# When the weight requests of the last two batches are issued, in an attention and soft-MoE kernel

## The chip, the core and the metric

The kernel runs on one core of a Trainium2 chip. The metric is the time of one execution on the device in microseconds (us). Engines named below: PE (TensorE: matrix products and transposes), DVE (VectorE), ACT (ScalarE), POOL (GpSimd), and SP (SyncE, which here only issues DMA requests). DMA requests issued by SP go to a queue that the profile calls q1, those issued by POOL to one called q0; both queues are served by the same 16 DMA engines.

## The reference

```python
# attention: B = 8 batches, H = 8 heads, S = 576 tokens, D = 64; 16 beacon keys/values ahead of the 576
scores = scale * q @ concat([beacon_k, k]).T          # causal mask on the 576, none on the beacons
a = softmax(scores);  attn = a @ concat([beacon_v, v])
# soft MoE over all N = 4608 tokens: Dm = 512, E = 8 experts x 4 slots, F = 1024
x = attn as [N, 512]
logits = x @ phi                                       # [N, 32]
d = softmax of logits over the tokens;  slot_input = d.T @ x      # [32, 512]
slot_out[e] = relu(slot_input[e] @ w1[e]) @ w2[e]
c = softmax of logits over the slots;   out = c @ slot_out        # [N, 512]
```

No expert can start before the attention of all 4608 tokens is done, since the slot inputs are sums over all tokens. The weights `w1` and `w2` are float32 in HBM, 2 MB each per expert, 33.5 MB in all; they do not depend on the attention and can be loaded at any time ahead of it.

## The kernel before, in words

**Pairs of heads.** The attention is written out as 32 pairs of heads, `n` = 0 to 31; `b, g = divmod(n, 4)` gives the batch and the pair in it. Two pairs form a half batch `m`; its keys and queries come in as two tiles `kstag` and `qstag` (L344, `load_qk`, one DMA of 576 KB each), are transposed on PE (`trps`, L492, for the very last half batch L496) and copied by DVE to `kT` and `qT`. One iteration of the loop at L759 issues, in an order written by hand for every engine (`manual_schedule`): four `scores` blocks of pair `n` (PE L523, exponentials on ACT L528, the causal mask on POOL, L514), the transposes of the next half batch, `attend` and `normalize` of pair `n-1`, and at fixed places the transposes of `x`, the logits and the slot sums of earlier batches. In the pairs with `g` = 1, 2, 3 the values of the next batch are cast (`cast_v`, POOL), and at `g` = 3 they are brought into their order in `vh`: POOL copies the last 80 tokens from `vrem` (L398), `perm_v` runs on PE, ACT (L411) and DVE, and POOL copies the beacons from `bvst` (L414).

**Loads of the inputs.** SP issues them two batches ahead: at `g` = 0 the values and the first half batch of keys and queries, at `g` = 2 the remainder of the values (`vrem`) and the second half batch, and one batch ahead the beacon values (`bvst`). Each waits for its buffer. The last of them, for batch 7, are requested in batches 5 and 6.

**Weights.** POOL issues them, since they are cast to 16 bits on the way. The list `wchunks` (L420) cuts `w1` and `w2` into 32 pieces of 512 KB (as 16 bits): both matrices of experts 0 to 4 first (20 pieces, resident in `w1h` and `w2h`), then `w1` of experts 5 to 7 (six), then `w2` of experts 5 to 7 (six). Experts 5 to 7 go into buffers that attention no longer needs: `wv` (expert 5) takes those of the values, `wt` (experts 6 and 7) those of the keys and queries. The very last piece is requested in two halves. `load_weights(count)` (L449) issues the next `count` pieces; it stands at the end of each pair (L798) and once more behind the loop (L801), where it issues whatever is left, after a POOL memset of the tile `siz`. POOL works in order, so a request stands behind every POOL instruction of its pair: the masks, the casts, and in the pairs with `g` = 3 the two copies into `vh`.

**After the pairs.** The last pair's `attend`, the last logits, the last slot sums; then the experts: `first(eg, fh)` (L829, `hps`, needs `w1`), `turn`, `second` (L850, `so`, needs `w2`), each for experts 0 to 3 and then 4 to 7. `second` of experts 4 to 7 uses the pieces of `w2` in the order of the list, the last piece last. Then `so1` is scaled by DVE (L874) and ACT (L877), and the output is computed and stored: `fps` on PE (L925), evictions on ACT (L930) and DVE (L932), DMA on SP (L936).

Of the kernel before, what the change touches and what calls it, by code (L numbers as in the profile page):

```python
# [268 lines left out]
def kernel(  # L269
# [118 lines left out]
    def cast_v(b, c):  # L388

        if c == 0:  # L390
            st["c", b] = work.tile([P, 4, H, D], F16, name="vc", tag="vc", bufs=1)
        if c < 2:
            for hs in (slice(4 * c, 4 * c + 2), slice(4 * c + 2, 4 * c + 4)):
                (nc.vector if c == 1 and b == 0 else nc.gpsimd).tensor_copy(  # L394
                    out=st["c", b][:, :, hs, :].rearrange("p t h d -> p h t d"),
                    in_=st["v", b][:, hs, :, :])
        else:
            nc.gpsimd.tensor_copy(out=vhs[b % 2][0:80, 4, :, 0:D], in_=st["r", b][0:80, :, :])  # L398
# [28 lines left out]
    def piece(e, m, j):  # L427

        if e < NRES:
            if m == 0:  # L430
                return w1h[e][:, 2 * j:2 * j + 2, :].rearrange("p t f -> p (t f)")
            return w2h[e][:, 4 * j:4 * j + 4, :].rearrange("p c d -> p (c d)")
        if (e, m, j) not in wtail:
            if e == NRES:
                t = stv.tile([P, 2, 2048], F16, name="wv", tag="v", bufs=2)
                for i in range(2):
                    wtail[e, m, i] = t[:, i, :]
            else:
                t = stq.tile([P, 2048], F16, name="wt", tag="kq"[len(wtail) % 2])
                wtail[e, m, j] = t[:, :]  # L440
        return wtail[e, m, j]
# [7 lines left out]
    def load_weights(count):  # L449
        for _ in range(count):  # L450
            if not wchunks:
                return
            e, m, j = wchunks.pop(0)
            if m == 0:
                nc.gpsimd.dma_start(
                    out=piece(e, m, j),
                    in_=moe_w1[e, 2 * j * P:2 * (j + 1) * P, :].rearrange("(p t) f -> p (t f)", t=2))
            else:
                src = moe_w2[e].rearrange("(p c) d -> p c d", c=NFC)
                cs = 2 if (e, m, j) == WLAST else 4  # L460
                for c in range(0, 4, cs):
                    nc.gpsimd.dma_start(
                        out=piece(e, m, j)[:, c * Dm:(c + cs) * Dm],
                        in_=src[:, 4 * j + c:4 * j + c + cs, :].rearrange("p c d -> p (c d)"))
# [10 lines left out]
    def transposes(m, which):  # L475

        b, hb = divmod(m, 2)
        t = st["kq"[which], b, hb]
        if which == 1:
            qTs[m] = work.tile([P, 2, S], BF, name="qT", tag="qT")  # L480
            dst = qTs[m][:, :, :]
        else:
            if m:
                beacon_keys(m)
            dst = kTs[m % 2][:, :, Nb:Nb + S]
        for j0, j1 in ((0, 5), (5, NJ)):
            tp = ps_tr.tile([P, j1 - j0, P], BF, name="trps", tag="tr")
            for j in range(j0, j1):
                for hh in range(2):
                    lo, hi = 64 * hh, 64 * hh + 64  # L490
                    if m < 2 * B - 1:
                        nc.tensor.transpose(tp[lo:hi, j - j0, :],  # L492
                                            t[:, hh, j, :].bitcast(BF)[:, 1::2], idb[:, :])
                        continue
                    for u in range(2):
                        nc.tensor.transpose(tp[lo:hi, j - j0, 64 * u:64 * u + 64],  # L496
                                            t[lo:hi, u, j, :].bitcast(BF)[:, 1::2],
                                            idb[lo:hi, lo:hi])
            do = dst.rearrange("p u (s j) -> p u s j", j=NJ)[:, :, :, j0:j1]
            ti = tp[:, :, :].rearrange("p j (u s) -> p u s j", u=2)  # L500
            if j0 and m == 0:
                nc.scalar.activation(do, ti, AF.Copy)
            else:
                nc.vector.tensor_copy(out=do, in_=ti)  # L504
# [12 lines left out]
    def scores(n, bank, masked=True):  # L517
        base, w, mms = BANKS[bank]
        sc = ps_sc.tile([P, 2, 512], FP, name="sc", tag="sc")
        for (c, q0, qw, col) in mms:  # L520
            for hh in range(2):
                po = 64 * hh
                nc.tensor.matmul(sc[:, hh, col:col + qw],  # L523
                                 kTs[n // 2 % 2][po:po + D, n % 2, c * P:(c + 1) * P],
                                 qTs[n // 2][po:po + D, n % 2, q0:q0 + qw], start=True,
                                 stop=True)
        ex = exps[n % 2]
        nc.scalar.activation(ex[:, :, base:base + w], sc[:, :, 0:w], AF.Exp, scale=scale)  # L528
        if masked:
            select(n, bank)  # L530
# [3 lines left out]
    def attend(n, hh):  # L534
        b, g = divmod(n, NG)
        h = head(n, hh)
        if hh == 0:
            pool, tag = (ps_av, "av") if n < NPAIR - 1 else (ps_sc, "sc")
            avs[n] = pool.tile([P, 2, 512], FP, name="av", tag=tag)
        av = avs[n][:, hh, 0:NC5 * DD].rearrange("p (i d) -> p i d", d=DD)  # L540
        for i in range(NC5):
            for c in range(i + 1):
                o = BLK[c, i]
                nc.tensor.matmul(av[:, i, :], exps[n % 2][0:KW[c], hh, o:o + P],  # L544
                                 vhs[b % 2][0:KW[c], c, h, :],
                                 start=(c == 0), stop=(c == i))
# [19 lines left out]
    def x_transposes(n):  # L566
        b, t = divmod(n, NG)
        tp = ps_tr.tile([P, S], F16, name="xtps", tag="tr")
        for i in range(NC5):
            nc.tensor.transpose(tp[:, QLO[i]:QLO[i] + QW[i]],  # L570
                                xs[b][0:QW[i], i, 2 * t:2 * t + 2, :].rearrange(
                                    "p h d -> p (h d)"),
                                idh[0:QW[i], 0:QW[i]])
        if n == NPAIR - 2:
            nc.scalar.activation(xT[:, t, 0:S], tp[:, :], AF.Copy)
        else:
            nc.vector.tensor_copy(out=xT[:, t, 0:S], in_=tp[:, :])  # L577
# [67 lines left out]
    def combine_T(b):  # L645

        dT = dTs[b]
        tp = ps_tr.tile([P, S], F16, name="etps", tag="tr")
        for i in range(NC5):
            nc.tensor.transpose(tp[:, QLO[i]:QLO[i] + QW[i]],  # L650
                                dT[0:QW[i], i, :, :].rearrange("p g s -> p (g s)"),
                                idh[0:QW[i], 0:QW[i]])
        nc.vector.tensor_copy(out=eT[:, b * S:(b + 1) * S], in_=tp[:, :])
# [25 lines left out]
    with tc.manual_schedule(engines={ET.PE, ET.DVE, ET.Activation, ET.Pool, ET.SP}):  # L679
# [79 lines left out]
        for n in range(2, NPAIR):  # L759
            b, g = divmod(n, NG)  # L760
            scores(n, 0)
            scores(n, 1)
            if n == 2:
                cast_v(1, 0)
            if n // 2 + 1 < 2 * B:
                transposes(n // 2 + 1, n % 2)
            attend(n - 1, 0)
            scores(n, 2)
            if n >= 3:
                x_transposes(n - 3)  # L770
            attend(n - 1, 1)
            if n >= 7 and g == 3:
                combine_T(b - 1)
            normalize(n - 1)
            scores(n, 3)
            if n == NPAIR - 1:
                x_transposes(n - 2)
            if b and g == 2:
                logits(b - 1)
            if n >= 8 and g == 0:  # L780
                dispatch(b - 2)
            if b + 1 < B and g:
                if b or g > 1:
                    cast_v(b + 1, g - 1)
                if g == 3:
                    perm_v(b + 1)
            if b + 1 < B and g == 0:
                load_bv(b + 1)
            if b + 2 < B:
                if g == 0:  # L790
                    load_v(b + 2)
                    load_qk(b + 2, 0)
                if g == 2:
                    load_vr(b + 2)
                    load_qk(b + 2, 1)
            if n == 5:
                nc.vector.tensor_copy(out=phih[:, :, :], in_=phif)
            load_weights((0, 1, 1, 1)[g] if b < 6 else 2)  # L798
        siz = work.tile([P, NDC, E * (NSL + SPE)], F16, name="siz", tag="qT")
        nc.gpsimd.memset(siz[:, :, :], 0.0)  # L800
        load_weights(len(wchunks))  # L801
# [174 lines left out]
```

## Time and profile before

| | before |
|---|---|
| median of 3 runs | 204.98 us (204.69 to 206.35) |
| the profiled execution: its own time | 204.81 us |
| its span in the profile | 203.1 us |
| PE, DVE, ACT, POOL busy | 78%, 66%, 66%, 59% of the span |
| DMA queue q1 (inputs and output): bytes, share of 16 engines | 38.01 MB, 52.9% |
| DMA queue q0 (weights): bytes, share of 16 engines | 16.78 MB, 41.5% |
| last matmul before / first transpose after the longest idle time of PE | 132.85 us / 142.38 us |
| first expert matmul (`hps`), end of `so`, end of span | 164.65, 173.85, 203.1 us |

All places in time are microseconds from the start of the span. The profile lists, for every engine, when it was busy and what ended each idle time before an instruction; the chain of work that ended last follows the program back from its end, at each step to what released it. A DMA request has an issue (on SP or POOL) and a landing, when its last part has arrived; its bytes move on 16 engines at once. The granted clock is the share of full speed at which PE was allowed to run.

### The profile page before, as it was taken

The numbers are of one execution on the slowest core, as the hardware profiler recorded it, in microseconds if no ns is written. First come the engines' busy times: TensorE is split into PE (matmuls) and PEld (weight loads), VectorE is DVE, ScalarE is ACT, GpSimd is POOL, SyncE is SP. The second block draws the span as 40 slices with busy tenths as digits, with TensorE's granted clock in tenths as the row PEclk, the third lists the DMA queues.
The fourth block names the chain that finished last, engine by engine and source line by source line (L and its number), as shares of the span: only waits on it lengthen the run. The fifth ranks groups of instructions, "written<-read, shape, count | busy, mean of one in ns | idle before, by whom it ended". The sixth has DMA issues, their size and how long they took to land.

```text
span 203.1 us, 7482 instructions
## 1 busy us (share of the span) xinstructions
PE 158.8 (78%) x3176; PEld 108.8 (54%) x3176; DVE 133.6 (66%) x281; ACT 134.1 (66%) x173; POOL 119.0 (59%) x269
## 2 busy tenths in 40 slices
PE   6687787898898989889889898900988999993300
PEld 2434555685675865667567586500867767741100
DVE  3446768888878987888887898710573733697400
ACT  2357868888888887898888888740289322692400
POOL 7028696697597588669759778801568600592000
PEclk9999999999999999999999999975599999997855
DMA  6999999999999999999999999995299994299992
GB/s 209 295 312 385 342 388 278 293 354 254 291 393 257 279 343 303 278 305 335 263 290 371 264 278 261 231 214 118 33 214 216 212 207 70 109 425 422 418 414 94
DMA packets 30646, 55.95 MB, mean 275 GB/s; under 512 B 8240, under 2 KB 16460, under 8 KB 30604
## 3 DMA queue, kind: packets, MB, share of 16 engines
q1 hardware_dynamic: 25564, 38.01, 52.9%
q0 software_dynamic: 4752, 16.78, 41.5%
q10 hardware_dynamic: 288, 0.59, 0.9%
q8 instruction: 27, 0.44, 0.8%
q14 instruction: 15, 0.12, 0.2%
HBM read 62.71 MB, written 9.44 MB: 355 GB/s over the span
## 4 chain that ended last, share of the span: by engine, by line
PE 57%; DMA 26%; ACT 7%; DVE 1%; issue 1%; POOL 1%; ACTq 0%; DVEq 0%; POOLq 0%
DMA kstag<-in_k_dram 20%; PE av L544 13%; PE sc L523 13%; PE trps L492 7%; PE xtps L570 5%; DMA out_dram<-osb 4%; ACT expT L528 4%; ACT vh L411 3%; PE fps L925 2%; PE vps L408 2%; PE lgps L589 2%; PE hps L833 2%; DMA qstag<-in_q_dram 2%; PE sips L628 2%; PE so L850 2%; PE vpt L408 1%
## 5 line engine op out<-in xcount | busy, mean ns | idle before, releaser
L528 ACT ACTIVATE expT<-sc 128x992 f16<-128x992 f32 (+3 forms) x128 | 104.7, 867 | 28.9 <-PE sc L523 28.1
L514 POOL TENSOR_SCALAR_AFFINE_SELECT expT<-expT 128x224 f16<-128x224 f16 (+3 forms) x128 | 55.1, 443 | 24.9 <-ACT expT L528 23.8
L523 PE MATMUL sc<-qT,kT 64*128 64x80 bf16 (+4 forms) x576 | 43.9, 247 | 10.7 <-ACT expT L528 5.8
L544 PE MATMUL av<-vh,expT 128*128 128x65 f16 (+1 forms) x960 | 40.8, 195 | 0.3 <-issue 0.3
L504 DVE COPY kT<-trps 128x640 bf16<-128x640 bf16 (+1 forms) x31 | 22.7, 773 | 21.9 <-PE trps L492 11.6
L544 PEld LDWEIGHTS <-expT 128*128 128x128 f16 (+1 forms) x960 | 34.1, 99 | 3.9 <-issue 1.1
L523 PEld LDWEIGHTS <-kT 64*128 64x128 bf16 x576 | 17.2, 96 | 27.7 <-issue 21.7
L504 DVE COPY qT<-trps 128x640 bf16<-128x640 bf16 (+1 forms) x31 | 22.7, 773 | 8.0 <-PE trps L492 6.3
L558 DVE TENSOR_TENSOR x<-av,r 128x640 f16<-128x640 f32 x32 | 26.4, 825 | 1.1
L394 POOL CAST vc<-vstag 128x512 f16<-128x512 f32 x30 | 17.9, 626 | 3.1 <-PE fill L664 3.1
L577 DVE COPY xT<-xtps 128x576 f16<-128x576 f16 x31 | 14.2, 457 | 5.0 <-PE xtps L570 5.0
L930 ACT ACTIVATE osb<-fps,rc 128x512 f32<-128x512 f32 (+1 forms) x19 | 11.5, 682 | 5.3 <-PE fps L925 4.2
L570 PE MATMUL xtps<-idh,x 128*128 128x128 f16 (+2 forms) x160 | 14.0, 218 | 0.1
L932 DVE TENSOR_SCALAR osb<-fps,rc 128x512 f32<-128x512 f32 (+1 forms) x18 | 12.2, 725 | 2.0 <-PE fps L925 1.3
L416 DVE CAST vh<-vpt 128x512 f16<-128x512 f32 x16 | 10.3, 685 | 2.9 <-PE vpt L408 2.9
L570 PEld LDWEIGHTS <-x 128*128 128x128 f16 (+2 forms) x160 | 9.1, 98 | 5.2 <-issue 4.9
L492 PE MATMUL trps<-idb,kstag 128*64 128x128 bf16 x270 | 10.7, 222 | 1.4 <-DMA kstag<-in_k_dram 1.4
L471 POOL COPY kT<-bkA 64x32 bf16<-64x32 bf16 x32 | 7.4, 231 | 7.0 <-DVE bkA L731 6.0
L925 PE MATMUL fps<-so,eT 128*128 128x512 f16 (+1 forms) x37 | 10.9, 421 | 0.5 <-DVE so L874 0.4
L492 PE MATMUL trps<-idb,qstag 128*64 128x128 bf16 x270 | 10.7, 222 | 0.8 <-DVE vh L416 0.5
L411 ACT ACTIVATE vh<-vps 128x1024 f16<-128x1024 f32 x8 | 8.2, 1027 | 4.6 <-PE vpt L408 4.6
L408 PE MATMUL vps<-vc,sel 32*128 32x512 f16 x64 | 9.6, 378 | 1.5 <-issue 0.8
(101 smaller groups left out, 193.1 us busy)
## 6 DMA issues: line engine op xcount, KB each, us to landing
kstag<-in_k_dram SPq DMA_DIRECT2D x15, 576.0 KB, 16.1
qstag<-in_q_dram SPq DMA_DIRECT2D x15, 576.0 KB, 14.1
out_dram<-osb SPq DMA_DIRECT2D x11, 768.0 KB, 8.8
vstag<-in_v_dram SPq DMA_DIRECT2D x7, 1024.0 KB, 11.8
w1h<-in_moe_w_dram POOLq DMA_DIRECT2D x10, 512.0 KB, 8.6
w2h<-in_moe_w_dram POOLq DMA_DIRECT2D x10, 512.0 KB, 8.5
wt<-in_moe_w_dram POOLq DMA_DIRECT2D x7, 512.0 KB, 8.1
wv<-in_moe_w_dram POOLq DMA_DIRECT2D x4, 512.0 KB, 10.6
```

The lines of the kernel that those rows point to most:

```text
L394: (nc.vector if c == 1 and b == 0 else nc.gpsimd).tensor_copy(out=st["c", b][:, :, hs, :].rearrange("p t h d -> p h t d"), in_=st["v", b][ ...
L408: nc.tensor.matmul(outs[c], sel[32 * c:32 * c + 32, t, :], vc[32 * c:32 * c + 32, t, :, :].rearrange("p h d -> p (h d)"), start=(t == 0), ...
L411: nc.scalar.activation(vhs[b % 2][:, 0:2, :, 0:D], ps[:, :, :].rearrange("p c (h d) -> p c h d", d=D), AF.Copy)
L492: nc.tensor.transpose(tp[lo:hi, j - j0, :], t[:, hh, j, :].bitcast(BF)[:, 1::2], idb[:, :])
L504: nc.vector.tensor_copy(out=do, in_=ti)
L514: nc.gpsimd.affine_select(out=ap, in_=ap, compare_op=AL.is_ge, fill=0.0, base=cbase, pattern=pat, channel_multiplier=-1)
L523: nc.tensor.matmul(sc[:, hh, col:col + qw], kTs[n // 2 % 2][po:po + D, n % 2, c * P:(c + 1) * P], qTs[n // 2][po:po + D, n % 2, q0:q0 + qw ...
L528: nc.scalar.activation(ex[:, :, base:base + w], sc[:, :, 0:w], AF.Exp, scale=scale)
L544: nc.tensor.matmul(av[:, i, :], exps[n % 2][0:KW[c], hh, o:o + P], vhs[b % 2][0:KW[c], c, h, :], start=(c == 0), stop=(c == i))
L558: nc.vector.tensor_tensor(out=xs[b][:, :, head(n, 0):head(n, 1) + 1:head(n, 1) - head(n, 0), :].rearrange("p i h d -> p h i d"), in0=av[:, ...
L570: nc.tensor.transpose(tp[:, QLO[i]:QLO[i] + QW[i]], xs[b][0:QW[i], i, 2 * t:2 * t + 2, :].rearrange("p h d -> p (h d)"), idh[0:QW[i], 0:QW ...
L925: nc.tensor.matmul(f[:, 0:hw], row_tokens(bb, j), so1[:, hw * i:hw * i + hw], start=True, stop=True)
```

## The change

One expression at the end of the loop over pairs:

```diff
-            load_weights((0, 1, 1, 1)[g] if b < 6 else 2)
+            load_weights((0, 1, 1, 1)[g] if b < 6 else (1, 1, 1, 2)[g] if b == 6 else 2)
```

Batches 0 to 5 are as before: no request behind a batch's first pair, one behind each other, 17 by the end of batch 5 (the loop begins with the third pair of batch 0). In batch 6 (pairs 24 to 27) there were two behind each pair; now there are one, one, one and two. In batch 7 (pairs 28 to 31) there are two behind each pair, as before. Before, the list was empty after one request behind pair 31 (piece 32, in its two halves). Now 30 pieces are requested by the end of the loop, and the two that remain are issued by `load_weights(len(wchunks))` at L801, behind the memset of `siz`, which found nothing left before. The order of the pieces, their sizes, their buffers and everything else are unchanged.

## The prediction

> **What bounds the kernel now.** I read the chain that ended last in order of time, then the waits of 100 to 150 us, then the DMA queues by stretch, then POOL's timeline.
>
> ```profile
> 110.30 0.58 PE trps L492 x17
> 110.89 31.45 DMA kstag<-in_k_dram
> 142.38 1.17 PE trps L496 x36
> ```
>
> Up to 110 us the chain is PE work in regular pairs: the key transposes of pair 24 start at 115.64 us, pair 25's query transposes at 119.41, so 3.77 us a pair. Then one load takes over, the last `kstag` (second half of batch 7), which was 31.45 us on its way. PE ends its last matmul ahead of it at 132.85 and stands still until 142.38.
>
> ```profile
> PEld L496 <- DMA kstag<-in_k_dram: 9.8, 1, 9.8
> POOL vh L398 <- DMA vrem<-in_v_dram: 7.6, 1, 7.6
> POOL vh L414 <- DMA bvst<-in_beacon_v_dram: 4.4, 1, 4.4
> ```
>
> POOL stands too: its two copies into `vh` wait for `vrem` (landed 139.06) and `bvst` (landed 144.0), and behind them stand pair 27's weight requests. All three loads are SP's, queue q1, requested by 118.7 us. What they shared the engines with is in the DMA queues of 128:132 (first pair of lines), 138:140 (second), 142:144 and 148:152 (one each):
>
> ```profile
> q0 software_dynamic: 197, 0.73, 90.2%
> q1 hardware_dynamic: 154, 0.19, 16.1%
> ...
> q0 software_dynamic: 88, 0.31, 77.7%
> q1 hardware_dynamic: 6, 0.01, 1.2%
> ...
> q1 hardware_dynamic: 25, 0.04, 4.9%
> ...
> q0 software_dynamic: 233, 0.83, 104.3%
> ```
>
> q0, the weights, fills the engines, and q1 creeps. The semaphore records tell how: fifteen of `kstag`'s sixteen completion steps are in by 128.6 us, the last comes at 142.3. So one DMA engine is far behind. On it the queues take turns: in 138:140 q1 gets 6 packets in 2 us, one per 0.33 us, and a 4096-byte weight packet takes 0.31 us (0.83 MB in 4 us over 16 engines). `vrem` is 640 runs of 256 bytes, 40 an engine, and each waits for a weight packet: 40 x 0.33 = 13.2 us, which is the way from 125.9 (the load ahead of it landed) to 139.06. When the weights stop, at 141 on this engine, q1 sends 2304-byte packets every 0.09 us.
>
> **The change part by part.** I number the weight pieces in their order; 17 are requested before batch 6. A piece is 0.524 MB, and 148:152 moves 0.83 MB in 4 us, so 2.5 us a piece with nothing beside it. Of POOL's requests before:
>
> ```profile
> 124.28 0.55 POOL L462 DMA_DIRECT2D w2h<-in_moe_w_dram  x1
> 124.82 0.54 POOL L455 DMA_DIRECT2D wv<-in_moe_w_dram  x1
> ...
> 128.65 0.55 POOL L455 DMA_DIRECT2D wv<-in_moe_w_dram  x1
> 129.19 0.54 POOL L455 DMA_DIRECT2D wt<-in_moe_w_dram  x1
> ...
> 144.10 0.61 POOL L414 CAST vh<-bvst 16x512 f16<-16x512 f32 x1 [4.43 <-DMA bvst<-in_beacon_v_dram]
> 144.66 1.08 POOL L455 DMA_DIRECT2D wt<-in_moe_w_dram  x2
> ```
>
> Before, pieces 18 to 23 went out with pairs 24 to 26 (119.4 to 129.2), and 24 to 32 from 144.66 on. Now 18, 19, 20 go out with pairs 24, 25, 26, pieces 21 and 22 behind pair 27's copies, and 23 to 30 two to a pair; 31 and 32 (32 is two requests of half size) follow pair 31 and the `siz` memset, 1.08 us, which before came after them.
>
> *Requests.* 33 of 0.54 us before and after; none is removed. POOL has three fewer (1.6 us) among pairs 24 to 26, where its idle gaps are 0.2 to 0.4 us before selects that wait for ACT; PE's pace is not POOL's there, so nothing to gain or lose. No new wait is written in the code. The memset moves forward; its reader is the DVE write at 163 us: nothing.
>
> *The late loads.* Pieces 21 to 23 leave the engine ahead of q1: 24 packets of 0.31 us, 7.4 us. If the engine never runs dry of weights, `bvst` lands at 144.0 - 7.4 = 136.6 and `kstag` at 135.0. But it does run dry. Piece 18 is done there near 125.2; piece 19 is now requested at 124.28, piece 20 at 128.65, and a request moves its first bytes 1.25 us later (144.66 to 145.91). Taking turns from 125.5: piece 19's eight packets take eight of `vrem`'s along (8 x 0.33, to 128.2). Then q1 is alone to 129.9: the 30 or so packets left of `vrem` at about 0.03 (0.33 less a weight packet) are 0.9 us, and in the other 0.8 go nine of `kstag`'s 16 at 0.09. Its last seven take turns with piece 20, 7 x 0.40: `kstag` lands near 133. The 16 of `qstag` behind it are 1.4 us, so `bvst` lands at 134.5. I take 133 for `kstag`, and for `bvst` 135, a little towards the bound.
>
> *Attention.* Pair 28 starts at 133.0 instead of 142.38: 9.4 us (bounds 7.4 and 9.5; PE is free at 132.85). The next pair also took 5.92 us (142.38 to 148.30) because the granted clock was 0.50 from 134.5 to 148; at 3.77 that is 2.15 more. PE would reach the last second-layer pieces (173.16 before) at 161.6, 11.5 earlier. What is late next is the weights.
>
> *The end of the weights.* POOL's copy of `bvst` now ends near 135.6, and pieces 21, 22 go out at 135.7 (floor 133.6: ACT's L411 ends at 132.42, the copy takes 0.61; ceiling 137.4, from `bvst` at 136.6). Before, nine pieces took from the request at 144.66 to the last landing at 171.0 (second half of piece 32, requested 160.05, 10.9 us): 26.3 us. Twelve take 3 x 2.47 more, 33.7. So the last weights land at **169.4**, only 1.6 us earlier (bounds 167.3 and 171.1). POOL's later requests stay ahead: pairs 28 to 31 ask by 149, the last at 151, while pieces flow to 169. Pieces 21 to 26, needed by the first layer near 156, land by about 154. So PE now waits in L850, where before it waited for no weights.
>
> *The rest.* Behind the last landing stand 13 of the L850 matmuls. Before, 88 took 2.54 us, 0.029 each; I take half clock, 0.058, as PE will have idled: 0.75 plus 0.27 for one to finish, so PE ends L850 at 170.4 against 173.85: **-3.4 us**. Bounds: at full clock -3.8; floor and ceiling of the restart move it by -2.1 and +1.7.
>
> *Output.* From there the kernel is bound by its stores, 0.79 MB each 1.9 us (425 GB/s), 0.62 us a tile of 256 KB. Even with `fps` at 0.43 us a tile PE keeps ahead; only the first tiles come later, **+0.3** (between 0 and 0.6).
>
> On the clock, the row first: PE went idle at 132.85 and the granted clock fell at 134.5, 1.7 us later, and it was back at 148.1, 5.7 us after work resumed. The Trainium skill, "TensorE: Matmul & The Clock Gate", Part 1: The HAM clock gate, speaks of an idle window of about 3.4 us before the clock halves. By that page, waits of 2.5 us from piece to piece would leave the clock full, and the sum would be -3.8 instead of -3.1. The row decides against it: 1.7 us was enough.
>
> **Sum.** -3.4 + 0.3 = -3.1 us on the profiled execution: 204.81 (span 203.1) becomes 201.7. The median of the runs is 204.98, 0.17 above it; I forecast **201.7**.
>
> **The rivals.**
>
> *The weights' tail overtakes (slower).* Three more pieces now stand behind the `bvst` wait, 7.4 us of q0 time at the end. If `bvst` does not come early enough, PE waits longer than it gained. The two balance when the last weights land at 172.5 (1.3 us before the old end), so when pieces 21, 22 go out at 138.8, `bvst` landing at 138.2. If `bvst` moved only half as far as the 7.4 us (140.3, as it would if the lagging engine were held by something other than the weights, such as the 16 KB instruction fetch on q8), the tail lands at 174.7: 207.0; if it did not move, 210.7. For: one engine alone is late, and no view says why. Against: q1's pace of one packet per weight packet, 0.33 us, and 0.09 us as soon as the weights stop. 0.10.
>
> *The change doesn't do what it says (same).* The late engine catches up 5 us and loses them at the end, between the two cases: 203 to 206, at 204.5. For: the DMA work is only moved, and both kernels end with the same bytes. Against: before, q0 stood idle from 142 to 146 while POOL waited, and the output could not start until 174. 0.12.
>
> *PE's chain decides (much faster).* If the weights kept up, the end moves by the full 11.5 us: 193.5. It needs twelve pieces in some 26 us, 2.2 us each; no stretch of the trace passes 0.86 MB in 4 us (2.44 us a piece). 0.03.
>
> *The forecast*, 199.6 (restart at its floor) to 203.5 (at its ceiling): 0.75.
>
> **How the numbers follow.** The range takes the forecast's bounds and reaches some way into the "same" case: 199.2 to 204.3. One per cent, 2 us, is about what a measurement of this kernel can tell from no change (three runs span 204.69 to 206.35). Faster by over 1%: nearly all of the forecast, 0.73, and 0.03; within 1%: 0.02 and 0.12; slower 0.10.
>
> **What the profile after would show.** Right: the wait PEld L496 on `kstag` shrinks from 9.8 us to under 2.5; L398 waits for no `vrem`; L414's wait ends near 135; the granted clock stays at 1.0 around 135 to 148; first `hps` near 153.6 instead of 164.65; a new wait of PE L850 on a DMA of `wt`, several us, and a half clock there; the last `wt` at 168 to 170.5; the stores still 425 GB/s. Wrong if: `kstag` is still late by 5 us or more with the weights gone; the pieces flow slower than 2.5 us; POOL blocks on a request because more than five are under way (the most seen before), and its selects come late; or the output at half clock falls behind its stores.

## The result, and the profile after

The changed kernel takes 202.17 us (median of six runs, 200.62 to 203.0) against 204.62 us for the kernel before beside it (six runs, 204.19 to 206.35): a ratio of 0.9864, 95% interval 0.9817 to 0.991. The profiled execution took 200.62 us (span 198.9) where that of before took 204.81 (203.1).

On two later chips the comparison came out at 1.0193 (1.0067 to 1.0319) and 1.0202 (1.0113 to 1.0292), so 2% slower, because it counts only executions near a kernel's fastest, and the kernel before has some there at 195 to 200.5 us beside about as many at 202.6 to 207.1. By medians these two chips have 201.62 us for the changed kernel against 201.24 and 200.75 against 202.82: no gain on the one, 1% on the other. What that spread is made of is the larger part of this study.

Where the time went in the profiled execution is in the waits and the chain that ended last. First the waits of the changed kernel (engine and line, what it waited for, us in total, times, longest):

```profile
PE so L850 <- DMA wt<-in_moe_w_dram: 3.2, 3, 1.7
```

The waits for `kstag`, `vrem` and `bvst` are gone, and this one is new. POOL's timeline around pair 27 (start, duration, what, idle time ahead and what ended it):

```profile
131.50 0.61 POOL L398 CAST vh<-vrem 80x512 f16<-80x512 f32 x1
132.60 0.61 POOL L414 CAST vh<-bvst 16x512 f16<-16x512 f32 x1 [0.49 <-ACT vh L411]
133.16 1.08 POOL L455 DMA_DIRECT2D wv<-in_moe_w_dram  x2
```

The DMA queues of 128:132 (two lines) and 132:136 (one; packets, MB, share of 16 engines):

```profile
q0 software_dynamic: 173, 0.64, 87.9%
q1 hardware_dynamic: 120, 0.11, 9.4%
...
q0 software_dynamic: 112, 0.39, 60.0%
```

q1 is empty by 132, and q0 runs with gaps for a few microseconds, until the new requests move. In POOL's timeline, POOL no longer stands: its copies follow ACT, and the weight requests of pair 27 go out at 133.16 instead of 144.66. Pair 28's key transposes start at 132.97 instead of 142.38. The end of the chain (start, duration):

```profile
150.72 0.95 POOL wt L462 x2
151.68 16.68 DMA wt<-in_moe_w_dram
168.40 0.60 PE so L850 x5
169.02 0.49 DVE so L874
```

Now the last half piece of the weights, requested at 151.68 and landed at 168.4, ends the experts. By stretch (length, busy time of PE, PEld, DVE, ACT, POOL with counts; then granted clock, DMA share, GB/s):

```profile
133.00:138.00 5.00, 5.00 (x165) 4.28 (x164) 3.98 (x8) 4.02 (x6) 4.42 (x11) 1.00 0.76 137
...
163.00:168.00 5.00, 2.07 (x43) 1.22 (x32) 0.00 (x0) 0.00 (x0) 0.00 (x0) 0.86 0.57 107
168.00:173.00 5.00, 4.51 (x31) 2.38 (x30) 2.47 (x4) 2.76 (x5) 2.97 (x2) 0.50 0.16 62
```

PE works through 133 to 138, where it stood before, at full clock. From 163 it waits for weights instead, and the output starts at half clock.

### The profile page after: what moved, and what is told of

Read it like the earlier page. It is cut to its first block, busy times and chain, and to the rows that moved or that the text cites. A ratio compares the mean times of both kernels' runs of the same rounds, so it can differ in the third digit from the quotient of the medians.

```text
span 198.9 us, 7482 instructions
## 1 busy us (share of the span) xinstructions
PE 161.8 (81%) x3176; PEld 108.6 (55%) x3176; DVE 133.8 (67%) x281; ACT 134.2 (67%) x173; POOL 118.5 (60%) x269
## 4 chain that ended last, share of the span: by engine, by line
PE 63%; DMA 14%; ACT 8%; DVE 3%; issue 2%; POOL 2%; ACTq 0%; DVEq 0%
PE av L544 16%; PE sc L523 15%; PE trps L492 9%; DMA wt<-in_moe_w_dram 8%; PE xtps L570 6%; PE fps L925 5%; ACT expT L528 4%; DMA kstag<-in_k_dram 4%; ACT vh L411 4%; PE vps L408 3%; PE vpt L408 2%; PE lgps L589 2%; DMA qstag<-in_q_dram 2%; PE sips L628 2%; DVE osb L932 2%
## 5 line engine op out<-in xcount | busy, mean ns | idle before, releaser
L523 PE MATMUL sc<-qT,kT 64*128 64x80 bf16 (+4 forms) x576 | 43.1, 244 | 10.8 <-ACT expT L528 5.9
L544 PEld LDWEIGHTS <-expT 128*128 128x128 f16 (+1 forms) x960 | 33.5, 97 | 4.8 <-issue 2.0
L925 PE MATMUL fps<-so,eT 128*128 128x512 f16 (+1 forms) x37 | 12.1, 456 | 0.4 <-ACT osb L930 0.2
L894 POOL TENSOR_SCALAR lo<-so 128x512 f32<-128x512 f16 x1 | 1.5, 1508 | 16.0 <-ACT so L877 16.0
L492 PEld LDWEIGHTS <-qstag 128*64 128x64 bf16 x270 | 8.4, 110 | 4.3 <-issue 4.2
## 6 DMA issues: line engine op xcount, KB each, us to landing
vstag<-in_v_dram SPq DMA_DIRECT2D x7, 1024.0 KB, 11.9
```

The lines of the kernel that those rows point to most:

```text
L492: nc.tensor.transpose(tp[lo:hi, j - j0, :], t[:, hh, j, :].bitcast(BF)[:, 1::2], idb[:, :])
L523: nc.tensor.matmul(sc[:, hh, col:col + qw], kTs[n // 2 % 2][po:po + D, n % 2, c * P:(c + 1) * P], qTs[n // 2][po:po + D, n % 2, q0:q0 + qw ...
L925: nc.tensor.matmul(f[:, 0:hw], row_tokens(bb, j), so1[:, hw * i:hw * i + hw], start=True, stop=True)
```

## The experiments

Two quantities decide below, and this table has them for every profiled execution. "Ahead" is the number of weight pieces requested in pairs 24 to 26, or at the start of 27, so ahead of POOL's copies; "end of `so`" is the start of L874 (L876 or L877 where the edit shifts lines). A load has landed when the last of its sixteen completion steps is in.

| kernel | ahead | `kstag` landed | `bvst` landed | last `wt` landed | end of `so` | time |
|---|---|---|---|---|---|---|
| before, in the prediction | 6 | 142.3 | 144.0 | 171.0 | 173.9 | 204.81 |
| before_again | 6 | 130.6 | 140.7 | 167.5 | 171.8 | 202.74 |
| before_third | 6 | 142.0 | 143.6 | 170.2 | 174.8 | 205.69 |
| keys_first | 6 | 126.5 | 141.6 | 168.5 | 173.0 | 204.0 |
| before_early | 8 | 126.4 | 136.3 | 164.0 | 165.3 | 196.17 |
| five_ahead | 5 | 138.6 | 140.2 | 169.7 | 171.3 | 202.24 |
| four_ahead | 4 | 136.7 | 138.4 | 170.4 | 170.8 | 201.75 |
| the changed kernel | 3 | 127.8 | 131.9 | 168.4 | 169.0 | 200.62 |
| after_again | 3 | 128.8 | 134.8 | 169.4 | 170.1 | 201.82 |
| after_third | 3 | 125.0 | 130.4 | 167.6 | 168.3 | 199.92 |
| without_last_three | 3 | 131.5 | 136.9 | 163.8 | 169.3 | 200.17 |
| early_request | 5 | 129.8 | 134.0 | 168.1 | 168.6 | 200.0 |
| early_third | 5 | 128.9 | 137.5 | 169.6 | 170.1 | 201.02 |
| none_ahead | 0 | 124.7 | 126.2 | 172.9 | 173.6 | 205.26 |

More pieces ahead go with later loads: `bvst` lands at 126.2 with none ahead, at 130.4 to 136.9 with three, at 138.4 and 140.2 with four and five that are requested behind the pairs, and at 140.7 to 144.0 with six. before_early, with eight, is the exception.

### Is the late `kstag` always there? (before_again)

The kernel before, unchanged.

> The kernel before, unchanged, for a second profile. Theory (weight packets hold up q1 on the one DMA engine that is furthest behind): the last kstag again lands at 140 to 144 us, with its last completion step more than 8 us behind the other fifteen, and PE waits 8 to 11 us for it. Rival (a late engine was a chance of that one execution): the landing differs by more than 3 us, the last step is not alone, and the time is the same anyway, so that the stall of PE is not what sets it.

Measured: 202.74 and 205.41 us. In the profile `kstag` lands at 130.6 and PE does not wait for it at all. The last completion step is 4.6 us behind the fifteenth, not more than 8: that expectation missed. Yet the time is only 2 us less. The waits of that profile say why:

```profile
POOL vh L414 <- DMA bvst<-in_beacon_v_dram: 7.6, 1, 7.6
...
PE av L544 <- POOL expT L514: 4.9, 2, 4.0
```

`bvst` is late (140.7, its fifteenth step at 136.0). POOL stands at its copy, and the causal masks of pair 28, which come later in POOL's order, are not done: PE's `attend` waits for them. So the price of the late loads does not need PE to wait for a load; POOL hands it on.

### Is it vrem's small packets that hold up kstag? (keys_first)

```diff
-                    load_vr(b + 2)
-                    load_qk(b + 2, 1)
+                    load_qk(b + 2, 1)        # for the last batch only
+                    load_vr(b + 2)
```

> The kernel before, but SP requests the last key and query loads ahead of the last vrem. Nothing of the weights is changed. Theory: the 40 small packets of vrem no longer stand ahead of kstag, each of which cost one weight packet of 0.33 us, so kstag lands about 13 us earlier, near 129, and PE starts pair 28 at 133 with no wait; but vrem and bvst land as late as before (139 to 144), so POOL's copies into vh end at 144.7 as before, PE then waits for vh in pair 29 (7 us), the weights restart at 144.7 and the last lands at 171: 202 to 204 us, at most 1.3% faster than before. Rival (the load is late because its engine is slow, whatever stands ahead of it): kstag lands at 139 or later, 204.6 us.

Measured: 204.61 us (204.0 to 205.17), beside 203.4 for the kernel before (196.57 to 206.45). PE has no wait for `kstag` (126.5, ahead of the 129 expected), and `vrem` and `bvst` land at 141.5 and 141.6:

```profile
POOL vh L398 <- DMA vrem<-in_v_dram: 11.2, 1, 11.2
...
PE av L544 <- POOL expT L514: 8.8, 2, 8.0
```

Some load is late in either order. That the order decides which one is not shown: `kstag` was on time in before_again too, with the order unchanged. PE's wait of 9.5 us for keys came back as 8.8 us for masks, and nothing was won: the expected 202 to 204 was too good, because I had counted the wait for `vh` and not the masks behind it.

### How many pieces may stand ahead? (five_ahead, four_ahead, none_ahead)

```diff
-            load_weights(... (1, 1, 1, 2)[g] if b == 6 else 2)
+            load_weights(... (2, 2, 1, 2)[g] if b == 6 else 2)     # five_ahead
+            load_weights(... (2, 1, 1, 2)[g] if b == 6 else 2)     # four_ahead
+            load_weights(... (0, 0, 0, 3)[g] if b == 6 else 3)     # none_ahead
```

> Two, two, one and two requests behind the pairs of batch 6: pieces 18 to 22 ahead of pair 27's copies, so one fewer than before and two more than in the changed kernel. Theory (each piece ahead costs the late loads 2.5 us, each piece behind costs the tail 2.5 us): against the changed kernel's profile kstag lands 5 us later, near 132.8, bvst near 137, POOL restarts at 137.6, ten pieces instead of twelve remain, so the last weights land near 168 and the time is that of the changed kernel within 1 us: 201 to 202.5. Rival (the loads are late as soon as the requests leave q0 no gap, however many pieces): kstag at 138 to 141, 203.5 to 205.

Measured: 200.91 us (200.36 to 202.24), beside 203.4 for the kernel before; about the time of the theory but not its landings: `kstag` at 138.6, `bvst` at 140.2, as the rival had it. The waits:

```profile
PEld L496 <- DMA kstag<-in_k_dram: 6.1, 1, 6.1
POOL vh L398 <- DMA vrem<-in_v_dram: 5.8, 1, 5.8
...
POOL vh L414 <- DMA bvst<-in_beacon_v_dram: 2.5, 1, 2.5
```

The last three completion steps of `kstag` come together here (138.0, 138.5, 138.6): it is not always one DMA engine that lags.

> Two, one, one and two requests behind the pairs of batch 6: one piece more ahead of pair 27's copies than in the changed kernel, eleven behind them instead of twelve. Theory: bvst lands up to 2.5 us later than in the changed kernel and the tail is one piece (2.5 us) shorter behind it: the time of the changed kernel within 1 us, 200.5 to 203. Rival (more distance of the requests is what counts, each piece less ahead is a gain): slower than the changed kernel by 1 us or more.

Measured: 201.28 us (200.41 to 202.02), beside 201.62 for the changed kernel on that chip: the same within 1 us, as expected. `bvst` landed 3.6 us later than in the changed kernel's profile beside it (138.4 and 134.8), where up to 2.5 was expected, and PE waits 4.7 us for `kstag`. Here the two paths meet, the one over POOL's copy and the one over the last weights:

```profile
POOL vh L414 <- DMA bvst<-in_beacon_v_dram: 6.2, 1, 6.2
...
PE so L850 <- DMA wt<-in_moe_w_dram: 0.6, 1, 0.6
```

> No request behind the first three pairs of batch 6 and three behind each from pair 27 on: fifteen pieces stand behind POOL's copies, none ahead. Theory (the tail of the weights is the price of the change): kstag, vrem and bvst land before 131, POOL restarts at its floor near 133, PE waits for no load of attention, and the last wt lands 15 x 2.5 us and 5 us behind the restart, near 176: 207 to 210, slower than the kernel before. Rival (less weight traffic beside the late loads is good without a price): 199 to 203.

Measured: 204.78 and 205.26 us, where the changed kernel has 201.62 and the kernel before 201.24 beside it, in the median; 3.4 us above the changed kernel. The loads land early (`bvst` at 126.2, all of its sixteen steps within 3.2 us), POOL asks for weights at 131.87, and nothing of attention waits for a load. Fifteen pieces behind that take 41.1 us, to 172.9. This is the mechanism of the prediction's slower rival, shown: pieces moved behind the copies come back at the end, here at 2.0 to 2.4 us each (41.1 us for fifteen against 33.9 to 35.2 for the changed kernel's twelve). The expected 176 was too late: it stood on a restart (POOL's first weight request behind its copies) at 133 and on 43 us for the tail. POOL's requests held something new:

```profile
142.44 0.56 POOL L462 DMA_DIRECT2D wv<-in_moe_w_dram  x1
143.03 0.53 POOL L462 DMA_DIRECT2D wt<-in_moe_w_dram  x1
145.64 0.53 POOL L462 DMA_DIRECT2D wt<-in_moe_w_dram  x1 [2.08 <-DMA wv<-in_moe_w_dram]
...
155.40 0.53 POOL L462 DMA_DIRECT2D wt<-in_moe_w_dram  x1 [1.91 <-DMA wt<-in_moe_w_dram]
155.92 1.08 POOL L800 MEMSET siz<- 128x1152 f16 x1
```

The request at 145.64 goes out when the piece requested eight earlier has landed (145.4), and so do the later ones (147.97 after 147.7, 150.41 after 150.1). With eight weight requests under way POOL stands at the ninth. The trace shows why: the weight requests use eight semaphores in turn, and each request waits on the semaphore that the one eight ahead of it signals. So this is an order in the program; a limit of the queue is not shown by it. The prediction had named it as a sign of being wrong, at more than five under way; in the changed kernel it does not occur. POOL's delay reaches the experts: the memset of `siz` behind it is late, and PE's first `hps` waits 4.3 us for `siz`.

### Is the tail of the weights all that is left? (without_last_three)

```diff
-    wchunks += [(e, 1, j) for j in range(2) for e in (5, 6, 7)]
+    wchunks += [(e, 1, 0) for e in (5, 6, 7)]
...
-        return piece(e, m, c // 4)[:, ...]
+        return piece(e, m, c // 4 if e < NRES else 0)[:, ...]
```

> The changed kernel without the last three weight pieces (second half of w2 of experts 5 to 7, whose products use the first half instead: that part of the result is left out). Theory (the tail of the weights sets the end of the experts): the last weights land 7.4 us earlier, near 161, PE gets there at about 161.5, the wait of L850 for wt is gone, 6 to 7.5 us faster than the changed kernel: 194 to 196. Rival (the wait for the weights hides a chain on PE, ACT or POOL that is nearly as late): at most 2 us faster, 199.5 or more.

Measured: 200.17 us in the profiled execution and 195.37 in the other. The profiled one speaks for the rival: the last weights land at 163.8, 5.5 us ahead of the end of `so`, L850 waits for no weights, and the end is where it was, 169.3.

```profile
POOL vh L414 <- DMA bvst<-in_beacon_v_dram: 4.0, 1, 4.0
```

`bvst` landed at 136.9 there, although only three pieces stood ahead, and attention was late by POOL again. The other execution, in the theory's range, has no profile; that its loads came in time is inferred from its time alone. With four_ahead, where both waits stand in one profile, the two paths are nearly equally long, and it seems that which is later differs from execution to execution.

### Does it repeat? (after_again, before_third, after_third)

> The changed kernel, unchanged, beside the others on one chip. From the five profiles so far: the kernel's time hangs on when bvst lands and POOL, standing at its copy into vh (L414), goes on. Theory: with twelve pieces behind that copy the end of the experts is the restart plus 35.8 us (133.16 to 169.0 in its first profile), so 200 to 203.5 us, with the last wt as the end of the wait in L850 and the restart between 133 and 136.5. Rival (PE's own chain sets it as in the kernel before, restart plus 30 us): L850 waits for no wt.

Measured: 201.62 us (200.85 to 202.88). The restart is at 135.44, the last weights land 34.0 us behind it, and the waits have both parts:

```profile
POOL vh L414 <- DMA bvst<-in_beacon_v_dram: 3.6, 1, 3.6
...
PE so L850 <- DMA wt<-in_moe_w_dram: 3.0, 3, 1.3
```

> The kernel before, unchanged, on the chip of the next three. So far its executions spread from 196.6 to 206.5 us, those of the changed kernel from 200.6 to 203.0. Theory (its time is POOL's restart behind bvst plus about 30 us to the end of the experts plus 31 to the end of the execution, and the restart wanders with how far one DMA engine lags behind): 196 to 207, spread over at least 4 us, and in the profile the end of so (L850) stands 29 to 31 us behind pair 27's weight request at L455. Rival (the spread is of the chip and hits every kernel alike): the two kernels beside it spread as far.

Measured: 204.31 us, 195.23 to 205.69 in six runs, with eleven more of the same kernel beside it from 195.69 to 207.1: median of the seventeen 202.82. The profile has the prediction's waits again:

```profile
PEld L496 <- DMA kstag<-in_k_dram: 9.7, 1, 9.7
...
POOL vh L398 <- DMA vrem<-in_v_dram: 9.1, 1, 9.1
```

The end of `so` stands 30.5 us behind the weight request of pair 27 (144.26 to 174.8), as expected. But it is not one engine that is far behind here: the last three completion steps of `kstag` come at 139.8, 140.4 and 142.0, the one ahead of them at 129.1.

> The changed kernel beside it. Theory (twelve pieces behind the restart, 35 to 36 us to the end of so, whatever PE does; a restart near 133 to 136): 200.5 to 203.5, a spread of 2.5 us or less, so 0.5 to 2% faster than the kernel before where that is at 204, and slower than its best executions. Rival: as wide a spread as the kernel before, and faster than it execution for execution.

Measured: 200.75 us, 198.82 to 202.32: a spread of 3.5 us where 2.5 was expected, with three of the six below the expected 200.5, against 11.9 for the kernel before on the same chip. The rival does not hold: the spread is not the chip's, and the changed kernel is not faster execution for execution.

### Requests ahead of POOL's copies (early_request, early_third, before_early)

```diff
+            if n == 27:
+                load_weights(2)              # ahead of the pair's masks and copies
...
-            load_weights(... (1, 1, 1, 2)[g] if b == 6 else 2)
+            load_weights(... (1, 1, 1, 0)[g] if b == 6 else 2)
```

> The changed kernel, but the two requests of pair 27 stand at the start of that pair, ahead of POOL's masks and of its two copies into vh, near 129 us instead of 133. Same pieces, same order. Theory (the weights' tail sets the end and q0 runs dry while POOL stands at the copies): q0 no longer idles between pieces 20 and 21 (about 3 us in the changed kernel's profile), the late loads pay at most 1 or 2 us for it, the last wt lands 2 to 3 us earlier: 198 to 200.5, 1 to 2 us or more below the changed kernel. Rival (the two pieces again hold up bvst packet for packet, 5 us): POOL restarts at 137 to 139 and the time is 202.5 to 205.

Measured: 199.32 us (199.25 to 202.36, five runs) beside 201.62 for the changed kernel. The DMA engines do not idle any more:

```profile
128.00:133.00 5.00, 5.00 (x116) 3.64 (x119) 3.90 (x11) 4.35 (x7) 4.86 (x13) 1.00 0.97 176
133.00:138.00 5.00, 4.39 (x121) 3.03 (x110) 4.45 (x9) 4.04 (x6) 3.64 (x9) 1.00 1.02 193
```

> The changed kernel with pair 27's two requests at the start of that pair. Theory (no idle q0 ahead of POOL's copies): 198.5 to 200.5, 1 to 1.5% faster than the changed kernel and with no execution above 203; in the profile no stretch of 128 to 143 us with a DMA share under 0.9. Rival (its first result was luck of where the lagging engine stood): 201 to 203.5, no better than the changed kernel.

Measured: 200.91 us (197.88 to 201.83), no better than the 200.75 beside it. In its profile `bvst` came at 137.5, POOL stood 5.7 us at its copy (to 137.62), and q0 ran dry after all:

```profile
138.00:143.00 5.00, 3.50 (x49) 2.68 (x50) 1.21 (x4) 1.17 (x2) 4.66 (x12) 0.55 0.40 61
```

So a gain of 1% is shown on one chip and not on the other: by these two profiles the two pieces save idle time where the loads are on time, and the saving is lost where `bvst` is late.

The same edit on the kernel before (two requests behind each pair, pair 27's moved to its start):

> The kernel before with pair 27's two requests at the start of that pair: two behind each pair as before, but these two do not stand behind POOL's copies; 24 and 25 join 18 to 23 ahead of the late loads. Theory (in the kernel before it is not the weights' tail that is late but attention, through POOL's copies and the masks behind them; two more pieces make bvst up to 5 us later): no gain, 203 to 208, L850 waits for no wt. Rival (an idle q0 behind the copies is what costs, as in the changed kernel): 199 to 201.5, about 1.5% faster than the kernel before.

Measured: 206.35 us in the median, and the widest spread of all, 196.17 to 209.34. The profiled execution is the fastest of them:

```profile
POOL vh L414 <- DMA bvst<-in_beacon_v_dram: 3.5, 1, 3.5
```

With eight pieces ahead, `bvst` landed at 136.3 and `kstag` at 126.4, earlier than with four or five; the experts ended at 165.3 and the time was 196.17. More pieces ahead go with late loads; they don't make them certain. Without the new wait for weights and with the late loads nearly on time, this is the fastest profile of all; the kernel before itself had executions at 195.2 and 195.7 us, which have no profile.

## Why the prediction was right, and what it did not see

**The late loads.** Pair 28 was to start at 133.0 and did at 132.97. `kstag` was put at 133, `bvst` at 135; they landed at 127.8 and 131.9, and at 128.8 and 134.8, 125.0 and 130.4 in the two repeats. The hand count with gaps in q0 came nearer than the bound without gaps (135.0 and 136.6). But it was worked out for one engine that is far behind, and in none of the three profiles is there one: the last completion step of `kstag` comes 0.1 to 0.9 us behind the fifteenth, where it was 13.7 in the prediction's. So the packet count itself was not tested, and `kstag` was put 4 to 8 us too late. The forecast did not suffer by it: pair 28 could not start before 133 by the prediction's own account, because PE was not free.

**The restart.** 135.7 was forecast with a floor of 133.6; it was 133.16, 135.44 and 133.70, the first a little below the floor.

**The weights' tail.** 169.4 was forecast; 168.4, 169.4, 167.6 were measured. "What is late next is the weights" is shown by the wait of L850 for `wt` in all three profiles. From the restart the tail took 35.2, 34.0 and 33.9 us where 33.7 was worked out.

**The rest of L850.** From the last landing to L874 it took 0.7 us, where 1.0 was summed. The end of `so` came 4.9 us earlier than before, not 3.4: the last landing 1.0 ahead of the sum, and about 0.4 in this term.

**The output at half clock.** The step was +0.3, and it is 0.7: from the end of `so` to the end of the execution it takes 30.9 to 31.0 us in the profiles that reach that point at full clock, and 31.6, 31.7 and 31.6 in those of the changed kernel. So -4.9 + 0.7 = -4.2, the difference of the two profiled executions, against -3.1 predicted. The choice of the half clock itself was right. Between 163 and 167 PE was busy for 1.2 us only, and the clock fell near 166.6. The Trainium skill, "TensorE: Matmul & The Clock Gate", Part 1: The HAM clock gate, gives one idle window of about 3.4 us, free-running. No single idle stretch here was longer than 1.7 us, so waits of that length, with a burst between them, do not keep the clock. The traces show more of it: in all fourteen profiles the time from one change of the clock to the next is a whole multiple of 3.41 us. In the 3.41 us that end with the fall at 166.61 PE was busy 0.96 us, and in those that end with the fall at 134.55 in the profile before 1.09 us. So PE need not stand still for a whole such stretch. The clock also fell at 152.96, where PE had been busy 3.04 of the 3.41 us; the runs do not show why.

**What it did not see.** The profile shown was one draw of a spread. Where PE's chain decides, the end of `so` stands 28.9 to 32.5 us behind `bvst`; where the weights decide, 0.5 to 0.7 behind the last landing; in every row of the table the end of the experts is one of the two. In the kernel before the first decides, and `bvst` wandered from 140.7 to 144.0 in its three profiles (136.3 with the eight ahead of before_early). The change took most of that away and put a nearly fixed tail in its place: all sixteen executions of the changed kernel lie between 198.8 and 203.0, median 201.6; forty of the kernel before between 195.2 and 207.1, median 203.9. The forecast of "faster by over 1%" is right for the chip that it was compared on and for the median of all executions; it is wrong on one of the two later chips, where the medians are within 0.4 us, and for the kernel before's best executions: nine of the forty lie under 199.5. On the chip of the comparison none of the six did, and that was luck for the forecast. No execution of the kernel before under 200 us has a profile; that its loads came in time there is inferred from before_early. The prediction priced "faster", "same" and "slower" as either-or: against a kernel that spreads like this all three occur.

**The rivals.** "The weights' tail overtakes" needed `bvst` at 138.2 or later with three pieces ahead. None of the four profiles with three ahead reached it, 136.9 in without_last_three coming nearest. As a mechanism it is shown by none_ahead. "PE's chain decides (193.5)" is not shown; the second execution of without_last_three, 195.37, with three pieces fewer at the end, speaks for it.

**What stays open.** Why one or a few DMA engines fall behind in one execution and not in the next. In the prediction's profile q1 gets one small packet for each weight packet on the lagging engine, and the packet records of 137.3 to 138.0 us have them 0.33 us apart; that explains how long a lag takes to work off, not how it began. The Trainium skill, "DMA: Bandwidth & Descriptors", Latency and other measured facts, states that two of the sixteen engines are usually slower and guesses at the fetching of descriptors for POOL's requests. That fits in so far as the loads were on time with no weight request beside them; the records here do not name the engines, and three steps lagged together in five_ahead and before_third. Whether a load order that spares the last loads altogether would bring 196 us every time was not tried.

## What to carry to other kernels

When two queues share saturated DMA engines, moving a load out of the way of a late one pays twice if an in-order engine stands behind that late load, because it releases that engine's masks and requests as well; but the bytes that were moved come back as a tail at the end, and the gain is the difference of the two. Before explaining a stall from one profile, take a second profile of the same kernel: here the named wait (`kstag`) was gone in the next one, and the same microseconds stood at another line. Where a time has two nearly equal last paths, read both of them from every profile and compare spreads as well as medians.

## What the runs showed of the hardware that was not expected

- One unchanged program on one core took 195.2 to 207.1 us in forty executions; no instruction differs. What differs between its three profiles, of 202.7 to 205.7 us, is when the last completion steps of its late loads arrive; its fastest executions have no profile.
- With eight weight requests under way on q0, POOL did not issue a ninth until the oldest had landed (none_ahead: 145.64 after 145.4, 155.40 after 155.1), about 2 us of POOL each: the program's requests share eight semaphores. Six more pieces behind the restart than in the kernel before are enough to meet this.
- The granted clock changes at whole multiples of 3.41 us from one change to the next, in every profile; it fell after 3.41 us in which PE was busy 0.96 and 1.09 us, with no single idle stretch over 1.7 us before the fall.
- At the end of the changed kernel's first profile eleven of the last half piece's sixteen completion steps come within 165.3 to 165.6 us, the other five at 166.3, 166.5, 167.5, 167.5 and 168.4. The landing that PE waits for is 2.8 us behind the eleventh step.
